# Stores on a second DMA queue, each held until a later load has landed, in an elementwise kernel

## Chip, cores, metric

The kernel runs on one core of one Trainium2 chip. The metric is the device time of one execution in microseconds (us), so smaller is better. Times are quoted as medians. A ratio is the mean time of one kernel's fast runs over the mean of the other kernel's fast runs of the same rounds, so it is not quite the ratio of the medians. Faster or slower needs 2%.

## The reference

```python
B, S, D = 512, 32, 640            # x, fx: bf16 [512, 32, 640]; alpha: one bf16 number
def reference(x, fx, alpha):
    return x + alpha * fx
```

Two tensors of 20.97 MB are read and one is written: 62.92 MB in all. There is almost no arithmetic.

## The kernel before

Each tensor is seen as 128 partitions by 81920 columns. It is cut into five chunks of 16384 columns, so a chunk is 4 MB and one of its rows is 32 KB. One VectorE instruction per chunk (`scalar_tensor_tensor`, called STT below) computes `x + alpha * fx` in place. There are four x tiles and two f tiles. All loads and stores are issued in one hand-made order on the sync queue (SP):

```python
    xs = ctx.enter_context(tc.tile_pool(name="xs", bufs=4))
    fs = ctx.enter_context(tc.tile_pool(name="fs", bufs=2))
    ...
    load_x(0)
    load_f(0)
    load_x(1)
    load_f(1)
    load_x(2)
    compute(0)
    load_f(2)
    store(0)
    load_x(3)
    compute(1)
    load_f(3)
    store(1)
    load_x(4)
    compute(2)
    load_f(4)
    store(2)
    compute(3)
    store(3)
    compute(4, 2)      # the last chunk in two halves
    store(4, 0, 2)
    store(4, 1, 2)
```

A transfer that needs a tile still in use waits on the sync queue, and everything behind it waits too. The order is chosen so that this never leaves the queue empty.

Of the kernel before, what the change touches and what calls it, by code (L numbers as in the profile page):

```python
# [1 line left out]

# [4 lines left out]

ACT = mybir.ActivationFunctionType
ALU = mybir.AluOpType
F32 = mybir.dt.float32  # L10
BF16 = mybir.dt.bfloat16

CHUNK = 16384


def alpha_to_lanes(nc, consts, psum, alpha, eng):

    P = nc.NUM_PARTITIONS
    a_1 = consts.tile([1, 1], alpha.dtype, name="a_1")
    eng.dma_start(out=a_1[:], in_=alpha[None, :])  # L20
    ones = consts.tile([1, P], alpha.dtype, name="ones")
    nc.vector.memset(ones[:], 1.0)  # L22
    a_ps = psum.tile([P, 1], F32, name="a_ps")
    nc.tensor.matmul(a_ps[:], ones[:], a_1[:], start=True, stop=True)  # L24
    a_f = consts.tile([P, 1], F32, name="a_f")
    nc.vector.tensor_copy(out=a_f[:], in_=a_ps[:])  # L26
    return a_f


@with_exitstack  # L30
def kernel(
    ctx: ExitStack,
    tc: tile.TileContext,
    x: bass.AP,
    fx: bass.AP,
    alpha: bass.AP,
    out: bass.AP,
):
    nc = tc.nc
    P = nc.NUM_PARTITIONS  # L40
    xv = x.flatten_outer_dims().rearrange("(p n) d -> p (n d)", p=P)
    fxv = fx.flatten_outer_dims().rearrange("(p n) d -> p (n d)", p=P)
    ov = out.flatten_outer_dims().rearrange("(p n) d -> p (n d)", p=P)
    F = xv.shape[1]
    K = F // CHUNK
    assert K * CHUNK == F and K == 5

    consts = ctx.enter_context(tc.tile_pool(name="consts", bufs=1))
    psum = ctx.enter_context(tc.tile_pool(name="psum", bufs=1, space=bass.MemoryType.PSUM))
    xs = ctx.enter_context(tc.tile_pool(name="xs", bufs=4))  # L50
    fs = ctx.enter_context(tc.tile_pool(name="fs", bufs=2))
    ctx.enter_context(tc.manual_schedule())

    a_f = alpha_to_lanes(nc, consts, psum, alpha, nc.scalar)
    xt, ft = {}, {}

    def load_x(k):
        xt[k] = xs.tile([P, CHUNK], x.dtype, tag="x", name="x_t")
        nc.sync.dma_start(out=xt[k][:], in_=xv[:, bass.ts(k, CHUNK)])  # L59

    def load_f(k):
        ft[k] = fs.tile([P, CHUNK], fx.dtype, tag="f", name="f_t")
        nc.sync.dma_start(out=ft[k][:], in_=fxv[:, bass.ts(k, CHUNK)])

    def compute(k, parts=1):
        n = CHUNK // parts
        for j in range(parts):
            s = bass.ts(j, n)
            nc.vector.scalar_tensor_tensor(  # L69
                out=xt[k][:, s],  # L70
                in0=ft[k][:, s],
                scalar=a_f[:],
                in1=xt[k][:, s],
                op0=ALU.mult,
                op1=ALU.add,
            )

    def store(k, j=0, parts=1):
        n = CHUNK // parts
        nc.sync.dma_start(  # L80
            out=ov[:, k * CHUNK + j * n : k * CHUNK + (j + 1) * n],
            in_=xt[k][:, bass.ts(j, n)],
        )

    load_x(0)
    load_f(0)
    load_x(1)
    load_f(1)
    load_x(2)
    compute(0)  # L90
    load_f(2)
    store(0)
    load_x(3)
    compute(1)
    load_f(3)
    store(1)
    load_x(4)
    compute(2)
    load_f(4)
    store(2)  # L100
    compute(3)
    store(3)
    compute(4, 2)
    store(4, 0, 2)
    store(4, 1, 2)


# [1 line left out]
_INS = ['x', 'fx', 'alpha']  # L109
_OUTS = [((512, 32, 640), 'bfloat16')]  # L110


# [23 lines left out]
```

## Time and profile before

The time was 152.45 us (three runs, 152.24 to 152.45). The profiled span was 150.6 us.

| what | before | where it is read |
|---|---|---|
| DMA engines busy | 98.0% of 16 engines' span | the page's table of DMA queues |
| mean rate over the span | 418 GB/s | same |
| VectorE busy | 86.9 us, 58% | the page's busy times |
| one 4 MB STT | 17.3 us | groups of instructions |
| one 32 KB row on one DMA engine | 1.21 us | packet records of the trace |

From the page of the kernel before: the busy shares of DVE (VectorE) and of the DMA engines in 40 equal slices of the span (tenths, 9 is 90% or more), the rate in each slice, and the table of DMA queues (packets, MB, share of 16 engines).

```profile
DVE  0000009999679998499991006999900089997000
...
DMA  6999999999999999799999999999999999999994
GB/s 200 444 453 435 418 418 418 418 444 453 444 453 435 418 418 418 339 444 470 418 418 418 418 418 435 435 435 453 426 435 444 418 418 435 435 435 405 426 444 205
...
q1 hardware_dynamic: 2304, 62.92, 98.0%
```

Read the DMA row first. It is 9 from the second slice to the last but one, with a single 7: the engines never run dry. VectorE has long holes, but they cost nothing: it is waiting for data from engines that are already full. At 1.21 us per 32 KB row an engine moves 27.0 GB/s and 16 engines move 432 GB/s, so the bytes alone take 145.6 us. Only about 5 us of the span is anything else.

From the waits of the same profile: who waited for whom, us in total, times, the longest.

```profile
DVE x_t L69 <- DMA f_t<-in_fx_dram: 49.5, 5, 20.6
```

This is the longest wait of a compute engine, and it is not a loss: the DMA engines are full meanwhile. It is the pace of the DMA stream, seen from VectorE.

### The profile page before, as it was taken

The page shows a single profiled execution, that of the slowest core. Times are in us where ns is not written, and L with a number is a line of the kernel's source. Part 1 is how long each engine was busy: PE and PEld are TensorE (multiplying, and loading weights), DVE is VectorE, ACT ScalarE, POOL GpSimd, SP SyncE. Part 2 cuts the span into 40 slices and gives each one's busy share as a digit, 9 for nine tenths or more (in the row PEclk, how much of TensorE's full clock was granted, in tenths as well). Part 3 has the DMA queues.
Part 4 walks back from the last instruction along what each step waited for, and adds up shares of the span by engine and source line. Part 5 has one row for each costly group of instructions (what it writes and reads, how often), then busy time and mean ns, then how long its engine had stood idle before and what let it go on. Part 6 is the DMA issues. An engine that isn't in the chain of part 4 may idle for free.

```text
span 150.6 us, 85 instructions
## 1 busy us (share of the span) xinstructions
PE 0.2 (0%) x1; PEld 0.1 (0%) x1; DVE 86.9 (58%) x8; POOL 0.2 (0%) x4
## 2 busy tenths in 40 slices
PE   0000000000000000000000000000000000000000
PEld 0000000000000000000000000000000000000000
DVE  0000009999679998499991006999900089997000
POOL 0000000000000000000000000000000000000000
DMA  6999999999999999799999999999999999999994
GB/s 200 444 453 435 418 418 418 418 444 453 444 453 435 418 418 418 339 444 470 418 418 418 418 418 435 435 435 453 426 435 444 418 418 435 435 435 405 426 444 205
DMA packets 2306, 62.92 MB, mean 418 GB/s; under 512 B 258, under 2 KB 258, under 8 KB 258
## 3 DMA queue, kind: packets, MB, share of 16 engines
q1 hardware_dynamic: 2304, 62.92, 98.0%
q10 hardware_dynamic: 2, 0.00, 0.0%
HBM read 41.94 MB, written 20.97 MB: 418 GB/s over the span
## 4 chain that ended last, share of the span: by engine, by line
DMA 56%; DVE 29%; DVEq 6%; issue 0%; SPq 0%
DMA f_t<-in_fx_dram 56%; DVE x_t L69 29%; DVEq L131 6%; SPq L59 0%; DVEq L69 0%
## 5 line engine op out<-in xcount | busy, mean ns | idle before, releaser
L69 DVE SCALAR_TENSOR_TENSOR x_t<-f_t,a_f,x_t 128x16384 bf16<-128x16384 bf16 (+1 forms) x6 | 86.6, 14439 | 49.5 <-DMA f_t<-in_fx_dram 49.5
L26 DVE COPY a_f<-a_ps 128x1 f32<-128x1 f32 x1 | 0.2, 159 | 1.1 <-PE a_ps L24 1.1
L22 DVE MEMSET ones<- 1x128 bf16 x1 | 0.2, 165 | 0.8 <-PEq L120 0.8
L24 PE MATMUL a_ps<-a,ones 1*128 1x1 bf16 x1 | 0.2, 159 | 1.9 <-DMA a<-in_alpha_dram 1.9
L120 POOL MEMSET const-bfloat16-1.0<- 128x1 bf16 x1 | 0.1, 102 | 0.0
L120 POOL MEMSET const-uint8-127<- 128x1 uint8 x1 | 0.1, 102 | 0.0
L24 PEld LDWEIGHTS <-ones 1*128 1x128 bf16 x1 | 0.1, 100 | 1.0 <-DVE ones L22 1.0
L120 POOL MEMSET const-float32-0.0<- 128x1 f32 x1 | 0.1, 99 | 0.2 <-issue 0.2
L120 POOL MEMSET const-float32-1.0<- 128x1 f32 x1 | 0.1, 99 | 0.0
## 6 DMA issues: line engine op xcount, KB each, us to landing
x_t<-in_x_dram SPq DMA_DIRECT2D x5, 4096.0 KB, 34.8
f_t<-in_fx_dram SPq DMA_DIRECT2D x5, 4096.0 KB, 32.1
out_dram<-x_t SPq DMA_DIRECT2D x4, 4096.0 KB, 36.5
out_dram<-x_t SPq DMA_DIRECT2D x2, 2048.0 KB, 15.2
a<-in_alpha_dram ACTq DMA_DIRECT2D x1, 0.0 KB
```

The costliest lines, as they stand in the source:

```text
L22: nc.vector.memset(ones[:], 1.0)
L24: nc.tensor.matmul(a_ps[:], ones[:], a_1[:], start=True, stop=True)
L26: nc.vector.tensor_copy(out=a_f[:], in_=a_ps[:])
L69: nc.vector.scalar_tensor_tensor(out=xt[k][:, s], in0=ft[k][:, s], scalar=a_f[:], in1=xt[k][:, s], op0=ALU.mult, op1=ALU.add,)
L120: nc = _bacc.Bacc("TRN2", target_bir_lowering=False, num_devices=1)
L131: with _tile.TileContext(nc) as tc:
```

## The change

The intent is to give loads the sync queue to themselves, with stores on the ACT queue. To keep the stores from slowing the loads that VectorE needs next, a store is held until a later load of fx has landed: store 0 until f1, store 1 until f2, store 2 until f3, stores 3 and 4 until f5. Store 5 needs no gate: its own STT waits for f5. The fifth chunk becomes two half chunks in loads, STT and stores (before, in STT and stores only). Cut to its core:

```diff
-CHUNK = 16384
+SIZES = [16384, 16384, 16384, 16384, 8192, 8192]
+GATE = [1, 2, 3, 5, 5, 5]
 ...
-    load_x(0)
-    ...                                   # one queue, the order shown above
-    store(4, 1, 2)
+    stores, landed = [], []
+    for k, c in enumerate(SIZES):
+        cols = slice(STARTS[k], STARTS[k] + c)
+        x_t = xs.tile([P, SLOT], x.dtype, tag="x", name="x_t")
+        nc.sync.dma_start(out=x_t[:, :c], in_=xv[:, cols])
+        f_t = fs.tile([P, SLOT], fx.dtype, tag="f", name="f_t")
+        landed.append(nc.sync.dma_start(out=f_t[:, :c], in_=fxv[:, cols]))
+        nc.vector.scalar_tensor_tensor(...)
+        stores.append(nc.scalar.dma_start(out=ov[:, cols], in_=x_t[:, :c]))
+    for k, s in enumerate(stores):
+        if GATE[k] > k:
+            tc.add_manual_dep(s, landed[GATE[k]], ...)   # wait for that load
```

More of the change, by code (lines that the diff above doesn't have):

```diff
@@ L11 @@
 BF16 = mybir.dt.bfloat16
-CHUNK = 16384
+SIZES = [16384, 16384, 16384, 16384, 8192, 8192]
+STARTS = [sum(SIZES[:k]) for k in range(len(SIZES))]
+SLOT = max(SIZES)
+GATE = [1, 2, 3, 5, 5, 5]
 def alpha_to_lanes(nc, consts, psum, alpha, eng):
@@ L44 @@
     F = xv.shape[1]
-    K = F // CHUNK
-    assert K * CHUNK == F and K == 5
+    assert sum(SIZES) == F
     consts = ctx.enter_context(tc.tile_pool(name="consts", bufs=1))
@@ L54 @@
     a_f = alpha_to_lanes(nc, consts, psum, alpha, nc.scalar)
-    xt, ft = {}, {}
-    def load_x(k):
-        xt[k] = xs.tile([P, CHUNK], x.dtype, tag="x", name="x_t")
-        nc.sync.dma_start(out=xt[k][:], in_=xv[:, bass.ts(k, CHUNK)])
-    def load_f(k):
-        ft[k] = fs.tile([P, CHUNK], fx.dtype, tag="f", name="f_t")
-        nc.sync.dma_start(out=ft[k][:], in_=fxv[:, bass.ts(k, CHUNK)])
-    def compute(k, parts=1):
-        n = CHUNK // parts
-        for j in range(parts):
-            s = bass.ts(j, n)
-            nc.vector.scalar_tensor_tensor(
-                out=xt[k][:, s],
-                in0=ft[k][:, s],
-                scalar=a_f[:],
-                in1=xt[k][:, s],
-                op0=ALU.mult,
-                op1=ALU.add,
-            )
@@ L78, in store @@
-    def store(k, j=0, parts=1):
-        n = CHUNK // parts
-        nc.sync.dma_start(
-            out=ov[:, k * CHUNK + j * n : k * CHUNK + (j + 1) * n],
-            in_=xt[k][:, bass.ts(j, n)],
-        )
-    load_x(0)
-    load_f(0)
-    load_x(1)
-    load_f(1)
-    load_x(2)
-    compute(0)
-    load_f(2)
-    store(0)
-    load_x(3)
-    compute(1)
-    load_f(3)
-    store(1)
-    load_x(4)
-    compute(2)
-    load_f(4)
-    store(2)
-    compute(3)
-    store(3)
-    compute(4, 2)
@@ L104 @@
-    store(4, 0, 2)
-    store(4, 1, 2)
+    stores, landed = [], []
[5 more added lines that the diff above has]
+        landed.append(nc.sync.dma_start(out=f_t[:, :c], in_=fxv[:, cols]))
+        nc.vector.scalar_tensor_tensor(
+            out=x_t[:, :c],
+            in0=f_t[:, :c],
+            scalar=a_f[:],
+            in1=x_t[:, :c],
+            op0=ALU.mult,
+            op1=ALU.add,
+        )
+        stores.append(nc.scalar.dma_start(out=ov[:, cols], in_=x_t[:, :c]))
@@ L109 @@
+    for k, s in enumerate(stores):
+        if GATE[k] > k:
+            tc.add_manual_dep(
+                s.ins if hasattr(s, "ins") else s,
+                landed[GATE[k]].ins.name if hasattr(landed[GATE[k]], "ins") else landed[GATE[k]].name,
+                mybir.DependencyInfo(mybir.DependencyClass.Sync, mybir.DependencyReason.DATA),
+                reason="store behind a later load",
+            )
 _INS = ['x', 'fx', 'alpha']
```

## The prediction

> **What bounds it now.** The DMA engines. The table of DMA queues gives q1 98.0% of the span of all 16 engines: 62.92 MB at a mean of 418 GB/s. DVE is busy 58%. The packet records show a 32 KB row at 1.21 us on each engine, for loads and stores alike: 27.0 GB/s an engine, 432 GB/s for 16. At that rate 62.92 MB is 145.6 us of the 150.6 us span. The other 5 us: first packet at 1.75 us, about 0.65 us of slower first packets, about 0.75 us lost near 59.5 us (at the first load-to-store change), about 0.3 us near 89.5 us, and 1.2 us after the last packet's end (149.4 us). The 49.5 us that DVE waits for f_t are only this stream's pace: the single queue never runs dry.
>
> **What the change does.** Same bytes. Stores leave the sync queue, so a load no longer queues behind a store; the fifth chunk becomes two halves. Two queues share the same 16 engines. The Trainium skill, "DMA: Bandwidth & Descriptors" (Issuing engines are not separate DMA queues), says that DMAs of different issuers interleave and only issue time is saved; that is 0.33 to 0.67 us an issue here, under transfers of 9.7 us, so nothing. The same page (Latency and other measured facts, row pitch) gives 214 GB/s per direction for copies on these queues, 428 in sum, so I expect mixed loads and stores to run at today's 432 or 1% less. No run of this case shows the mix yet.
>
> **What is on the critical path.** I replayed the program order with 9.7 us per 4 MB, 17.3 us per STT, two tiles of f and four of x, and even sharing. Loads stay queued until the last: f5 waits for the STT of chunk 3 (about 118 us) while half loads and store 2 keep the engines busy. It lands about 129 to 131 us. Store 3, ready since about 118 us, is gated on exactly that load, as is store 4. So both queues are empty once: last load packet to landing 0.5 us, issue to first packet 1.0 us, slow first packets 0.6 us, engines' skew up to 0.6 us: 2 to 2.7 us with DMA near zero. Then stores 3 and 4 (14.5 us) cover the last STT (8.75 us). The old kernel has no such gap: its stores 2 and 3 stand queued behind the last load. Start and end cost the same. Mixing adds 0 to 1.5 us.
>
> So 152.45 + about 2.2 (gap) - 0.4 (load-to-store hiccups changing) = **154.2 us**, 8 in 10 between **152.3** and **157.0**. Faster by over 2%: 0.03; within 2%: 0.76; slower by over 2%: 0.21.
>
> **What would show it.** Bytes unchanged, split over q1 (42 MB) and q10 (21 MB), their shares summing to about 96%. The DMA row at 9 except one dip of about 2 us near 128 to 133 us, where the ACT queue's wait for f_t ends. Loads beside a store take about twice 9.7 us. The chain ends in: f_t landing, store issue, stores. Mixed stretches at 425 to 432 GB/s.
>
> **What would make it wrong.** (1) Mixed reads and writes exceed 432 GB/s: some us faster; at today's rate the span's floor is about 148.5 us, so over 2% faster needs this. (2) Each load-to-store change costs 0.75 us like the first: interleaving makes dozens, and over 2% slower follows. (3) Uneven sharing (16 KB rows beside 32 KB) delays f5, but stores fill the time. (4) A gate opens another gap that I took as covered.

## The result, and the profile after

The change takes 154.0 us (four runs, 153.94 to 154.11) against 152.45 us (152.24 to 152.72) of the kernel before in the same rounds. The ratio is 1.0101, with a 95% interval of 1.0084 to 1.0119: about 1.5 us longer, and "same" by the 2% rule. The profiled span is 152.2 us, 1.6 us longer.

From the page of the changed kernel, the same lines as before; q1 is the sync queue, q10 the ACT queue.

```profile
DVE  0000009999589996000999940049999499795000
...
DMA  7999999999997999999999999999999999699994
GB/s 215 448 422 422 422 413 430 465 456 422 422 396 319 474 448 439 413 413 413 430 474 456 430 413 413 422 418 478 413 418 435 422 439 413 276 413 413 422 469 211
...
q1 hardware_dynamic: 1728, 41.94, 65.1%
q10 hardware_dynamic: 866, 20.97, 32.1%
```

The bytes are the same, now on two queues. The DMA row has one new mark: a 6 in slice 35, at 276 GB/s, which is near 129 to 133 us. The other low slice (319 GB/s, near 46 to 49 us) has its twin in the kernel before (339 GB/s, near 60 to 64 us).

From the timeline of the changed kernel around that slice (start us, length us, engine, line, what; the count is of merged instructions, so a length can cover waiting).

```profile
118.44 0.33 SPq L64 DMA_DIRECT2D f_t<-in_fx_dram  x1
120.65 8.75 DVE L65 SCALAR_TENSOR_TENSOR x_t<-f_t,a_f,x_t 128x8192 bf16<-128x8192 bf16 x1 [2.24 <-DMA f_t<-in_fx_dram]
130.34 9.15 ACTq L73 DMA_DIRECT2D out_dram<-x_t  x3
130.37 8.75 DVE L65 SCALAR_TENSOR_TENSOR x_t<-f_t,a_f,x_t 128x8192 bf16<-128x8192 bf16 x1 [0.96 <-DMA f_t<-in_fx_dram]
```

The last load, f5, is issued at 118.44 us and has landed by about 130.3 us. At 130.34 us, not before, the ACT queue begins to issue its last three stores, the first of which has had its result since 118.43 us. Busy time by stretch shows what the engines did meanwhile (columns: stretch, its length, busy us of PE, PEld, DVE and POOL, granted clock, DMA share, GB/s). First the kernel before, then the changed one.

```profile
64.00:88.00 24.00, 0.00 (x0) 0.00 (x0) 15.53 (x1) 0.00 (x0) 1.00 1.00 430
104.00:118.00 14.00, 0.00 (x0) 0.00 (x0) 5.00 (x1) 0.00 (x0) 1.00 1.01 438
129.90:131.10 1.20, 0.00 (x0) 0.00 (x0) 1.20 (x1) 0.00 (x0) 1.00 1.01 437
```

```profile
64.00:88.00 24.00, 0.00 (x0) 0.00 (x0) 15.93 (x1) 0.00 (x0) 1.00 1.01 434
104.00:118.00 14.00, 0.00 (x0) 0.00 (x0) 14.00 (x1) 0.00 (x0) 1.00 1.02 439
129.90:131.10 1.20, 0.00 (x0) 0.00 (x0) 0.73 (x1) 0.00 (x0) 1.00 0.00 0
```

The first two lines are stretches that, in the changed kernel, hold stores mixed with loads (in the first, from 66 to 76 us, loads alone). The rate is the same, 434 and 439 against 430 and 438 GB/s. Differences of a few GB/s mean nothing here: a start one microsecond later (105 to 118 us) gives 421 against 444. The stretches that store 0 and store 1 fill with loads beside them, 48 to 65 and 76 to 93 us, both ran at 432 GB/s. The third is the loss: for 1.2 us no DMA engine moves a byte.

The packet records account for the whole span. I sorted them as follows, as a mean over the 16 engines in us: "full speed" counts 1.213 us for each 32 KB row and 0.611 us for each 16 KB row; "slower packets" is what single packets took beyond that (over 0.05 us); "idle" is the rest up to the end of the last packet, which includes the engines' skew (they do not all end their last load at the same moment).

```
                          before   change
first packet starts         1.73     1.73
rows at full speed        145.63   145.78
slower packets              1.79     1.77
idle                        0.27     1.63
last packet to the end      1.19     1.33
span                      150.61   152.24
```

Of the 1.63 us that the span grew, 1.36 us is idle time. Half rows add 0.15 us (two 16 KB rows take 1.222 us, one 32 KB row 1.213 us). The rest, 0.14 us, is at the end of the span.

### The profile page after: what moved, and what is told of

Same layout as the page of the kernel before. It is cut to its first block, busy times and chain, and to the rows that moved or that the text cites. A ratio compares the mean times of both kernels' runs of the same rounds, so it can differ in the third digit from the quotient of the medians.

```text
span 152.2 us, 93 instructions
## 1 busy us (share of the span) xinstructions
PE 0.2 (0%) x1; PEld 0.1 (0%) x1; DVE 87.0 (57%) x8; POOL 0.2 (0%) x4
## 3 DMA queue, kind: packets, MB, share of 16 engines
q1 hardware_dynamic: 1728, 41.94, 65.1%
q10 hardware_dynamic: 866, 20.97, 32.1%
## 4 chain that ended last, share of the span: by engine, by line
DMA 61%; DVE 28%; SPq 1%; issue 0%; DVEq 0%
DMA f_t<-in_fx_dram 61%; DVE x_t L65 28%; SPq L62 1%; SPq L64 0%; DVEq L65 0%
```

## The experiments

The theory: the gate lets both queues run empty once, from the end of the last load to the first packet of store 3, and that gap is on the critical path. Rivals: mixing loads and stores costs time; the half chunks or the second queue cost time; the gates as such are the loss.

### 1. The last three stores on the sync queue

```diff
+        xt.append(x_t)
+        if k < 3:
             stores.append(nc.scalar.dma_start(out=ov[:, cols], in_=x_t[:, :c]))
+    for k in (3, 4, 5):
+        c = SIZES[k]
+        nc.sync.dma_start(out=ov[:, STARTS[k] : STARTS[k] + c], in_=xt[k][:, :c])
```

> The change, with its last three stores moved to the sync queue behind the last load of fx and no gate on them; stores 0 to 2 stay gated on the ACT queue. Theory (the empty queue between the landing of the last load and the first packet of store 3 is the loss): the DMA gap of about 1.7 us near 130 us goes, 152.2 to 152.7 us, as before the change. Rival (two queues, mixed loads and stores, or the half chunks cost it): the mixing and the halves are all still there, so about 154.0 us.

Measured: 152.5 us, ratio to before 0.9963 (0.9933 to 0.9993). The same stretch around 130 us:

```profile
129.90:131.10 1.20, 0.00 (x0) 0.00 (x0) 0.91 (x1) 0.00 (x0) 1.00 1.01 437
```

The gap is gone and the loss with it. The mixing of stores 0 to 2, the gates on them and the half chunks are all still there, so none of those is the main cost.

### 2. The first three stores on the sync queue

```diff
         landed.append(nc.sync.dma_start(out=f_t[:, :c], in_=fxv[:, cols]))
+        j = k - 2
+        if 0 <= j < 3:
+            nc.sync.dma_start(out=ov[:, STARTS[j] : STARTS[j] + SIZES[j]], in_=xt[j][:, : SIZES[j]])
 ...
-        stores.append(nc.scalar.dma_start(out=ov[:, cols], in_=x_t[:, :c]))
+        xt.append(x_t)
+        if k >= 3:
+            stores[k] = nc.scalar.dma_start(out=ov[:, cols], in_=x_t[:, :c])
```

> The change, with stores 0 to 2 on the sync queue in the places that the old kernel gave them, so that loads and stores are never mixed before the gate; stores 3 to 5 stay on the ACT queue behind the last load. Theory (gap): the gap stays, 153.8 to 154.3 us. Rival (mixing costs): about 152.5 us, as before the change.

Measured: 154.29 us, ratio 1.0088 (1.0055 to 1.012). Nothing is mixed any more, the gap remains, and so does the loss. The same stretch in this run:

```profile
129.90:131.10 1.20, 0.00 (x0) 0.00 (x0) 0.04 (x1) 0.00 (x0) 1.00 0.03 14
```

Together with the first experiment this separates the two causes: the loss goes with the gap, not with the mixing.

### 3. The gap made longer

```diff
+        if k == 3:
+            a_2 = consts.tile([1, 1], alpha.dtype, name="a_2")
+            extra = nc.scalar.dma_start(out=a_2[:], in_=alpha[None, :])
         stores.append(nc.scalar.dma_start(out=ov[:, cols], in_=x_t[:, :c]))
 ...
+    hold(extra, landed[5])      # the 2-byte load waits for f5
+    # and stores 3, 4, 5 also: hold(s, extra)
```

> The change, with a 2-byte load of alpha put on the ACT queue that waits for the last load of fx, and stores 3 to 5 waiting for it too: the wait is lengthened, no bytes worth speaking of are added. The first such load takes about 1.2 us from issue to landing in the trace. Theory (the empty queue is on the critical path, microsecond for microsecond): gap 1.7 to about 3.0 us, 155.1 to 155.6 us. Rival (the gap is hidden): 154.0 us.

Measured: 155.53 us, ratio 1.0164 (1.0135 to 1.0193). Between the last load packet's end and the first packet of store 3 there are now 2.6 us, against 1.3 us. Busy time by stretch of this run:

```profile
129.90:132.50 2.60, 0.00 (x0) 0.00 (x0) 1.84 (x1) 0.00 (x0) 1.00 0.00 0
```

A gap 1.3 us longer makes the kernel about 1.4 to 1.5 us longer (155.53 against 154.0 to 154.13 us for the change in its own runs; those were on other chips). Experiment 2, with the gap of 1.3 us, ran in the same rounds as this one, and this one is 1.24 us longer. Within this noise the gap counts microsecond for microsecond.

### 4. No gates at all

```diff
-GATE = [1, 2, 3, 5, 5, 5]
+GATE = [0, 0, 0, 0, 0, 0]
```

> The change with every gate taken away (a store waits for its own STT alone). Replayed with packets of the two queues taken in turn, as the trace of the change shows them, stores 3 and 4 then take about half of the packet turns from loads x5 and f5, f5 lands near 144 us instead of 130, and the last STT (8.75 us) has nothing to hide behind: an empty stretch of about 10 us before store 5. Expect no gap at 130 us, one of 9 to 11 us near 144 to 155, and 161 to 164 us. Rival (gates are nothing but the loss): 152.4 us.

Measured: 162.92 us, ratio 1.065 (1.0613 to 1.0687). Timeline and busy time by stretch of this run:

```profile
121.18 8.75 DVE L65 SCALAR_TENSOR_TENSOR x_t<-f_t,a_f,x_t 128x8192 bf16<-128x8192 bf16 x1 [2.56 <-DMA f_t<-in_fx_dram]
144.98 8.75 DVE L65 SCALAR_TENSOR_TENSOR x_t<-f_t,a_f,x_t 128x8192 bf16<-128x8192 bf16 x1 [15.05 <-DMA f_t<-in_fx_dram]
```

```profile
129.90:131.10 1.20, 0.00 (x0) 0.00 (x0) 0.03 (x1) 0.00 (x0) 1.00 1.01 437
144.50:154.50 10.00, 0.00 (x0) 0.00 (x0) 8.75 (x1) 0.00 (x0) 1.00 0.02 7
```

There is no gap at 130 us. But stores 3 and 4 have taken turns with the last loads, the last STT starts at 144.98 us instead of 130.37 us, and while it runs for 8.75 us there is nothing left to move. So some holding back of the last stores is right. The fault of the change is only the way: a wait for the landing empties the queue, while a place behind the load in the same queue (experiment 1) keeps the order without a pause.

### 5. The first three gates taken away

```diff
-GATE = [1, 2, 3, 5, 5, 5]
+GATE = [0, 0, 0, 5, 5, 5]
```

> The change with the gates of stores 0 to 2 taken away and those of stores 3 to 5 (behind the last load) kept. Replayed: the engines never run dry before 129 us either way, so these three gates buy nothing and cost nothing: one gap of about 1.7 us near 130 us, 153.8 to 154.3 us. Rival (the early gates protect the loads and pay for themselves): 155.5 us or more.

Measured: 154.93 us, above the stated range, on a chip where the kernel before scattered more (152.16 to 153.92 us). The ratio 1.0127 (1.0087 to 1.0166) overlaps that of the change (1.0084 to 1.0119). The gap is there (DMA share 0.07 between 129.9 and 131.1 us). The rival's 155.5 us is not reached. The packet records show where the excess of this run sits: all engines together are empty for the same 1.34 us, but they end their last loads 1.23 us apart, against 0.54 us in the change, so the idle time per engine is 2.4 us against 1.6 us. In experiment 2 it is the same (1.15 us apart, 2.4 us idle). Whether the missing early gates cause the wider skew, and so are worth a few tenths of a microsecond, stays open.

### 6. The repeat, side by side

The first experiment and the change, unchanged, on one chip with more rounds.

> The first experiment again, unchanged, beside the change on one chip, with more rounds: does it really beat the kernel before, as its 0.9963 said? If the gap is the whole loss it ties with the kernel before or is ahead by at most 0.5%: ratio 0.995 to 1.001.

> The change itself, on the same chip as the repeat of the first experiment: ratio to before 1.008 to 1.013, so 1.0 to 1.3% behind that repeat.

Measured: the first experiment's kernel 152.43 us, ratio to before 0.9986 (0.9969 to 1.0003); the change 154.13 us, ratio 1.0097 (1.0078 to 1.0116). Their difference, 1.7 us, is the cost of the gated tail. Idle time in the packet records is 0.1 us per engine in the one and 1.9 us in the other. The tail on the sync queue brings the change level with the kernel before; the 0.4% lead of the first run was not confirmed.

### 7. A side question: the slow packets ahead of the first store

Every kernel above loses about 0.8 to 1.1 us per engine to slow packets around the time when its first store starts. Busy time by stretch, kernel before and then the change:

```profile
57.00:62.50 5.50, 0.00 (x0) 0.00 (x0) 2.79 (x2) 0.00 (x0) 1.00 0.97 352
```

```profile
42.00:48.00 6.00, 0.00 (x0) 0.00 (x0) 5.59 (x1) 0.00 (x0) 1.00 0.97 350
```

The DMA engines are 97% busy in both stretches but move only about 350 GB/s. If that could be moved under the slow first packets at the start, a kernel would, by estimate, gain about 0.8 us. I tried small early writes, on the ACT queue ahead of the load of alpha: one of 128 pieces of 512 B into `out` (in the kernel before, and in the kernel of experiment 1), the same into a scratch tensor, and one of 640 pieces that touches every 32 KB piece of `out`.

```diff
+    w_t = consts.tile([P, 256], x.dtype, name="w_t")
+    nc.vector.memset(w_t[:], 0.0)
+    nc.scalar.dma_start(out=ov[:, 0:256], in_=w_t[:])   # or scratch[:, :], or 5 pieces a row
     a_f = alpha_to_lanes(nc, consts, psum, alpha, nc.scalar)
```

> The kernel before, with a 64 KB write of zeros (128 rows of 512 B) into columns of out that store 0 overwrites later, issued on the ACT queue at the start. It asks about the stretch of slow packets (about 0.85 us per engine) that the trace of every kernel so far has just ahead of its first store. Guess A (it belongs to the first write into out): it moves into the first few us, where the first packets are slow anyway; 0.5 to 1.0 us less than before, about 151.7 us. Guess B (it belongs to the first large store, or to a change of direction): it stays, 152.4 to 152.6 us.

> The first experiment (last three stores on the sync queue behind the last load) with the same early write. Guess A: 151.5 to 151.9 us, the fastest of all. Guess B: 152.2 to 152.5 us.

> Control of the early write: the kernel before with the same 64 KB write going to a scratch tensor in HBM instead of out. If the slow packets belong to the first write into out itself, they stay (152.4 to 152.6 us); if to the first write of the execution at all, they go here too (about 151.7 us).

> The kernel before with an early write of zeros that touches 512 B in each 32 KB row piece of out (640 pieces, 328 KB), so that every stretch that a later store writes has been written once. If the slow packets ahead of the first store belong to places of out not written before, they go (excess near 58 to 61 us under 0.2 us per engine, against 0.85 us); if not, they stay as with the smaller early write.

Measured: 153.06, 152.94 and 152.96 us for the first three (ratios 1.0018, 1.0007 and 1.0015, all intervals containing 1), and 173.34 us in one run for the last. On the chip of the first three the kernel before took 152.81 us, so the microseconds stated for guess B were missed too; only the ratios can be read. The slow packets stayed in all four: about 0.8, 1.0, 1.0 and 1.35 us per engine, by the packet records. Guess A fell: a small early write to those places does not take them away. What they are stays open.

The fourth run failed for another reason, and it is worth seeing. From its page, DMA issues (KB each, us from issue to landing), and from its waits:

```profile
out_dram<-w_t ACTq DMA_DIRECT2D x1, 320.0 KB, 50.9
...
PE a_ps L24 <- DMA a<-in_alpha_dram: 52.2, 1, 52.2
```

A write of 320 KB took 50.9 us, about as long as the five loads of 4 MB that the sync queue held at the start, and the load of alpha stood behind it. Its 640 pieces are 40 for each of the 16 engines. In the packet records they start from 5.9 us to 50.9 us, so one piece per engine about every 1.15 us, close to the time of one 32 KB row. Between the first and the last of them 586 rows of the loads started. So while the sync queue had work, an engine gave each queue about one row in turn, whatever the row's size. The change shows the same: from 104 to 118 us, 126 store rows of 32 KB started beside 123 load rows of 16 KB.

## Why the prediction was right

- **The time.** Predicted 154.2 us (152.3 to 157.0), measured 154.0 us. The class "within 2%" was given 0.76 and came.
- **The bound.** Right: the changed kernel still moves the same bytes at the same rate, and the DMA table's shares sum to 97.2% (predicted about 96%).
- **Mixing is neither gain nor loss.** Right: 434 and 439 GB/s mixed against 430 and 438 GB/s before, and experiment 2 took the mixing away without gain. The Trainium skill, "DMA: Bandwidth & Descriptors" (Issuing engines are not separate DMA queues), says that the queues share the same engines; this trace agrees (65.1% and 32.1% of the same 16 engines). The 214 GB/s per direction that the prediction took from the same page (Latency and other measured facts, row pitch) is for copies between HBM tensors. Twice that, 428 GB/s, is only an estimate for this mix; the trace gives 432.
- **The gap.** Right in place and cause, a little too large in size. Predicted 2 to 2.7 us with f5 landing at 129 to 131 us; it landed at about 130.3 us, and idle time grew by 1.36 us. From the last load packet's end (129.84 us) to the issue (130.34 us) took 0.5 us and from there to the first packet (131.18 us) 0.84 us. The slow first packets that I added (0.6 us) did not come: store 3's first packets took 1.23 us, against 1.21.
- **The -0.4 us for load-to-store changes.** Wrong: slower packets cost 1.79 us before and 1.77 us after. Nor did the sum hold the half rows (0.15 us) and the end of the span (0.14 us). The forecast growth was 2.2 - 0.4 = 1.8 us. The gap took 0.84 us less than that sum has for it, the credit fell short by 0.38 us, and the two forgotten terms added 0.29 us, which makes the 1.63 us that the span grew. The mechanism was right; that the total came so close is partly luck, because these errors offset each other.
- **Even sharing.** Only partly right. The engines share by rows, not by bytes (experiment 7), so a half chunk's 16 KB rows get a third of the bytes beside 32 KB rows. In the change this stayed harmless, as the prediction's third caveat said; without gates (experiment 4) it is part of why f5 comes so late (from 122 to 137.5 us, 137 load rows of 16 KB beside 128 store rows of 32 KB). The loads f2 and f3, beside a store, took about 16 and 15 us from first to last packet, not twice 9.7 us. One reason is that stores 0 to 2, issued while loads filled the engines, sent their first packet only 4.5, 3.9 and 3.4 us after the issue, against 0.84 us for store 3 with the engines empty.
- **Two signs did not show.** The waits of the ACT queue list nothing, so the gate cannot be read there. And the chain of waits does not run through the stores. In the changed kernel it ends in the last STT, and before the change it ends on VectorE too:

From the chain of the changed kernel, its last piece (start us, length us, what).

```profile
130.37 8.75 DVE x_t L65
```

That STT ends at 139.12 us and releases store 5, but stores 3 and 4 still occupy the engines until about 146 us. The chain follows who released the last issue; it does not see that the issue then stood in a queue. For a DMA-bound kernel the DMA row by slices and the stretches are the views to trust.

## What to carry to other kernels

In a kernel whose DMA engines are already 98% busy, moving transfers to another queue brought nothing (experiment 6: ratio 0.9986 with no gap), and a wait for a landing that left both queues empty cost its full length: here 0.5 us to notice and 0.84 us to start again, plus skew. If a store must come after a load, put it behind the load in the same queue rather than behind a semaphore on its landing. Two busy queues shared an engine row by row here, so a transfer of small rows beside one of large rows was served at the pace of the large rows.

## What the Trainium skill lacked or had wrong

- "DMA: Bandwidth & Descriptors" (Queues, rings and completion order) says that an engine drains a whole packet, typically 9 to 17 descriptors, from one ring before it switches. Here the turn was about one row, of 512 B, 16 KB or 32 KB alike: 40 pieces of 512 B per engine took 45 us beside 32 KB rows. A 4 MB load is 8 rows and one 4-byte record on each engine, so a turn of 9 would have been a whole load. The page does not warn that a small-row transfer beside a large-row one is slowed to that pace (320 KB in 50.9 us).
- The same page (Anatomy of one DMA) gives a fixed cost of about 2.0 us for the gpsimd path; for the sync and ACT queues the page has only a first-byte latency of about 0.6 us (Specifications). "SBUF — State Buffer" (The DMA setup-cost knee) gives the 2 us for every DMA. Here, on these queues, last packet to dependent issue plus issue to first packet was 1.34 us (0.50 and 0.84).
- No page that I found says how long a transfer waits on one queue while the other fills the engines: 3.4 to 4.5 us from issue to first packet for stores 0 to 2 of the change.
- No page that I used has the slow packets around the first store of an execution: 0.8 to 1.1 us per engine in the kernels timed here, unmoved by a small early write.
